# Attention followed by a Fourier mixing layer on one core: the middle channel's rank-one products on 32-row tiles of TensorE, in one visit a batch

## The chip, the cores and the metric

The kernel runs on one core of one Trainium2 chip. The metric is the device time of one execution in microseconds (us); several runs give a median. The engines are named as in the profile: PE is TensorE's matrix multiplication and PEld its weight load, DVE is VectorE, ACT is ScalarE, POOL is GpSimd, SP is SyncE, which here only issues DMAs. L1267 is line 1267 of the kernel before; the changed kernel's lines differ by up to some fifty and are named as such.

## What is computed

Eight batches (B = 8) of 576 tokens, 8 heads of 64, so 512 columns a token. Each batch goes through an attention without a token-by-token matrix, then through a Fourier mixing layer with a residual, a LayerNorm and a two-layer network, all in float32:

```python
q_s = softmax(q, axis=-1); k_s = softmax(k, axis=2)
kv = np.einsum('bhsd,bhse->bhde', k_s, v)
x = np.einsum('bhsd,bhde->bhse', q_s, kv)      # then (B, S, H*D) = 8 x 576 x 512
mixed = np.real(np.fft.fft(np.fft.fft(x, axis=1), axis=2))
u = x + mixed
un = (u - mean(u)) / sqrt(var(u) + 1e-6)
out = u + np.maximum(un @ w_ch1, 0) @ w_ch2     # 512 -> 2048 -> 512
```

## The kernel before, in words

**The two layers.** Nearly all of TensorE's time goes to the two matrix products of the network, which use Strassen's scheme of seven products per level (`ORDER`, products 1, 6, 5, 7, 2, 4, 3). `up` (L1544) makes the first layer of a batch, `down` and `deep_down` (L1641, L1671, L1760) the second. In `deep_down`, which serves the later groups, a unit of the scheme has seven products n, each 16 passes of 128 columns; product 1 and 2 go to the PSUM bank `ba`, 6, 7 and 4 to `bb`, 5 and 3 to `bc`. Each of the three banks exists once. After a product its `ends` step reads the bank: `plus` (L1678, on VectorE) adds bank and a kept sum into `u2`, `u3` or an output. The next product into `bb` can begin only when VectorE's read of the one before is done. The steps `a_step` (L1617) form the scheme's sums of left operands on VectorE, and some on GpSimd. A float32 product counts as two passes (two weight loads and two matmuls) on TensorE.

**The Fourier transform** is made of products with tables of cosines and sines. It uses the symmetries of the real transform: rows are folded, and of the 512 columns five blocks of spectrum channels remain, k = 0 to 4. Blocks 0 and 1 are cosines, 2 and 3 sines, of 128 (127) channels each; block 4 (`KT`) is the single middle channel.

- *First stage*, along the tokens: for batches 2 to 7 `blocks(b)` has, for each k, `own(k)` (L1207, the main products, 144 or 145 columns), `tails` (L1234, ten small products with 16 or 17 rows on 32-row tiles of TensorE, the last two for k = 4), and `copies` (L1246, L1249, L1250, on ScalarE) out of the PSUM tiles `two` into SBUF: `Z` for the batch's own channels, `ZT` for the rows shared by a pair of batches, and for the middle channel row 0 of `Zr` (own, 256 wide) and of `ZTr` (shared). All other rows of `Zr` and `ZTr` are zero. In L1207, `own(4)` uses 128 weight columns though one channel is wanted. Batch 0 has its own steps in the opening, batch 1 uses `block(1, k)`.
- *Second stage*, along the columns: `second()` for an own half c = 0 or 1 of the batch, or (odd batches) for the shared rows. `times` makes four products with the table `cd` (L1264) and, added into the same bank, the middle channel's product (L1267), whose left operand `Zr` or `ZTr` is 128 rows of which only row 0 isn't zero. `copy` (L1273, ScalarE) brings the sine half to SBUF, `sums` (L1281, L1282, VectorE) forms sum and difference of the halves, and `added` (L1294, L1295, VectorE) adds them to x in two halves, for each of the one or two row blocks.
- Then `norm` (L1321 and on), the transposes of the normalized rows (L1382) and the copies L1390 that lay out `unT`, the left operand of the next `up`.

**The order of the work** is written out by hand: each step has a time, the steps of all parts are sorted by it, and each engine then executes its instructions in that order (`manual_schedule`). A time decides order only; waits come from data and from buffers. The opening has a list of its own (`OPENING`), where the steps `m0` and `m1` are the second stage of batch 0. For batches 2 to 7 `timed` places it: the first stage from the start of the second layer on, and the mixes at

```python
for i, some in enumerate(mixes):
    steps += at(t + 9.7 + 1.65 * soon + 3.2 * i, some)
```

so that TensorE visits the second stage two times in even batches and three times in odd ones (in batch 7 the shared rows first), with Strassen products in between: in batches 3 and 5 the first visit comes after the 16 passes of product 1, the second in the middle of product 5, the third in the middle of product 2.

Of the kernel before, what the change touches and what calls it, by code (L numbers as in the profile page):

```python
# [40 lines left out]
F32 = mybir.dt.float32  # L41
# [5 lines left out]
P = 128  # L47
B, H, S, DH = 8, 8, 576, 64
D = H * DH
# [85 lines left out]
def paired(t):  # L135
    return t.rearrange("p (q a) -> p q a", a=2)


class _Block:
    def __init__(self, ctx, tc, q, kT, v, w1, w2, ft, cd, out):  # L140
# [27 lines left out]

        self.Zr, self.ZTr = c.tile([P, HD], F32, name="Zr"), c.tile([P, P], F32, name="ZTr")
        for t in (self.Zr, self.ZTr):  # L170
            nc.gpsimd.memset(t[:], 0.0)
        self.kb = c.tile([P, NR, 4, NC * Q], F32, name="kb")
# [427 lines left out]
    def opening(self, fetch, converted):  # L600
# [40 lines left out]
        for c in range(2):  # L641
            named(f"m{c} times,m{c} copy,m{c} sums,m{c} add0,m{c} add1", self.mix_own(0, c))
        tiles = [f"{c}{u}" for c, u in ((0, 0), (0, 1), (1, 0), (1, 1))]
# [502 lines left out]
    def block(self, b, k):  # L1146
# [26 lines left out]
        def copies():  # L1173
            pz, Z = box.pop(), self.Z[b]
            z, zt = (self.Zr[0:1], self.ZTr[0:1]) if k == KT else (Z[0:n, k, :], self.ZT[0:n, k, :])
            nc.scalar.copy(paired(z), interleaved(pz[:, NT - 1:NT - 1 + 2 * ME])[:, 0:P, :])

            at = W * (b % 2)
            nc.scalar.mul(paired(zt[:, at:at + Q]), interleaved(pz[:, 0:2 * MO])[:, 0:NT - 1, ::-1],
                          -1.0 if sines else 1.0)  # L1180
            nc.scalar.copy(paired(zt[:, at + Q:at + W]), interleaved(pz[:, 0:2 * ME])[:, NT - 2::-1, ::-1])
# [3 lines left out]
    def blocks(self, b):  # L1185
# [51 lines left out]
        def copies(k, part, copy=nc.scalar.copy):  # L1237
            n, sines, Z = {3: QD - 1, 4: 1}.get(k, P), k in (2, 3), self.Z[b]
            z, zt = (self.Zr[0:1], self.ZTr[0:1]) if k == KT else (Z[0:n, k, :], self.ZT[0:n, k, :])
            flat = box[sines][0:n].rearrange("p a n -> p (a n)")  # L1240
            odd, even = place(k, 1).start, D + place(k, 0).start

            def both(x, y, size, step=1):
# [4 lines left out]
            w = W * (b % 2)  # L1248
            nc.scalar.mul(paired(zt[:, w:w + Q]), both(even, odd, NT - 1), -1.0 if sines else 1.0)  # L1249
            nc.scalar.copy(paired(zt[:, w + Q:w + W]), both(even + NT - 1, odd + NT - 2, NT - 1, -1))  # L1250

        return own, tails, copies, early, sine

    def second(self, z, zr, adds, two=True, apart=None):

        nc, V = self.nc, self.nc.vector
        cd, box = self.cd, []

        def times():
            banks = apart() if apart else [self.acc((P, D), two)] * 2  # L1260
            parts = (1, 0, QD), (0, QD, QD + 1), (2, NN + QD - 1, QD), (3, NN, QD - 1)
            for k, at, size in (parts[2], (3, HD, QD), *parts[:2]) if apart else parts:
                rows, pm = QD - 1 if k == 3 else P, banks[k > 1]
                nc.tensor.matmul(pm[:, at:at + size], lhsT=z(k)[0:rows], rhs=cd[0:rows, at:at + size], start=True,  # L1264
                                 stop=(k != 0))
                if k == 0:
                    nc.tensor.matmul(pm[:, at:at + size], lhsT=zr(), rhs=cd[:, D:], start=False, stop=True)  # L1267
            box.extend(banks)

        def copy():  # L1270
            sn = self.sn[self.turns % 2]
            self.turns += 1
            nc.scalar.copy(paired(sn[:, 0:HD]), interleaved(box.pop()[:, HD:]))  # L1273
            box.append(sn)

        def sums():
            pm, sn = box
            two = self.halves()
            a = interleaved(pm[:, 0:2 * (QD + 1)])[:, 0:QD, :]
            for i, op in enumerate((ALU.subtract, ALU.add)):  # L1280
                V.tensor_tensor(out=paired(two[:, i * NN + 1:(i + 1) * NN]), in0=a, in1=paired(sn[:, 1:NN]), op=op)  # L1281
            V.tensor_copy(two[:, ::NN], pm[:, QD:QD + 1].to_broadcast([P, 2]))  # L1282
            box.append(two)

        steps = [(0, times), (2.6, copy), (3.6, sums)]
        for i, add in enumerate(adds):
            steps.append((5 + 1.2 * i, lambda add=add: add(box[2][:, 0:NN], box[2][:, NN:])))
        return steps
# [7 lines left out]

    def mix_shared(self, p):
        return self.second(lambda k: self.ZT[:, k, :], lambda: self.ZTr[:],
                           [lambda lo, hi: self.added(self.xshared(p), hi, lo)])

    def mix_own(self, b, c):
        s = slice(c * P, (c + 1) * P)
        adds = [lambda lo, hi: self.added(self.xpart(b, c, 0), lo, hi, of=None if b or c else self.kept), lambda lo, hi: self.added(self.xpart(b, c, 1), hi, lo, None if b else self.nc.gpsimd)]
        def apart():
# [5 lines left out]
        return self.second(lambda k: self.Z[b][:, k, s], lambda: self.Zr[:, s], adds, apart=None if b else apart)  # L1310

# [522 lines left out]
def kernel(ctx: ExitStack, tc: tile.TileContext, q, kT, v, w1, w2, ft,  # L1834
# [3 lines left out]
    def timed(t, order, g):  # L1838
# [155 lines left out]
```

## Time and profile before

| what | value |
|---|---|
| three runs | 1005.66, 1005.86, 1006.8 us; median 1005.86 us |
| profiled execution | span 1006.6 us (the profile gives no time outside its span) |
| granted clock of TensorE | 9 tenths or more in each of 40 slices |
| busy: PE, PEld, DVE, ACT, POOL | 99%, 85%, 71%, 49%, 44% of the span |
| DMA | 236.37 MB, 235 GB/s in the mean |

How to read it: the span runs from the first to the last instruction of one execution. In a timeline, a row is a run of like instructions that follow each other: start in us, length in us, engine, line, operation, output and input tiles with their shapes, and how many; in square brackets the idle time ahead of it and what ended it. Two rows of one engine can overlap, since instructions are pipelined: the pace of an engine is read from the starts, not from the lengths. The ends of PE rows are modelled.

### The profile page before, as it was taken

What the parts mean: (1) busy time and instruction counts of PE and PEld (TensorE: products, weight loads), DVE (VectorE), ACT (ScalarE), POOL (GpSimd) and SP (SyncE); (2) the same over time, 40 slices, a digit from 0 to 9 for tenths busy, and PEclk for the clock granted to TensorE, in tenths of its full rate; (3) what the DMA queues carried; (4) which work ended last, traced back from release to release, by engine and by line L of the source; (5) the groups of instructions that cost most, each with busy time, mean ns of one, the idle gap of its engine ahead of it and who ended that gap; (6) DMA issues with size and microseconds to landing.
All of it is one profiled execution on the core that took longest, in us unless ns stands there. A gap on an engine that the chain in (4) does not pass through costs nothing.

```text
span 1006.6 us, 19808 instructions
## 1 busy us (share of the span) xinstructions
PE 995.6 (99%) x7562; PEld 855.7 (85%) x7562; DVE 718.6 (71%) x1356; ACT 493.2 (49%) x1277; POOL 442.9 (44%) x445
## 2 busy tenths in 40 slices
PE   8999999999999999999999999999999999999998
PEld 6844464888888899889988998899889998998897
DVE  6898898666765887588756877688667945685563
ACT  4585642872468228832775177625772342151200
POOL 4263420357535637664655465655646450040000
PEclk9999999999999999999999999999999999999999
DMA  9987499687989666975677577847753765674573
GB/s 300 258 281 245 158 240 346 205 243 226 342 283 272 230 230 219 266 237 210 251 220 242 206 269 237 253 174 270 231 204 135 267 213 200 224 265 172 183 256 132
DMA packets 123559, 236.37 MB, mean 235 GB/s; under 512 B 24184, under 2 KB 88440, under 8 KB 112840
## 3 DMA queue, kind: packets, MB, share of 16 engines
q1 hardware_dynamic: 123096, 234.58, 71.0%
q8 instruction: 60, 0.98, 0.4%
q14 instruction: 35, 0.29, 0.1%
q10 hardware_dynamic: 288, 0.26, 0.1%
q0 software_dynamic: 80, 0.26, 0.1%
HBM read 199.94 MB, written 39.06 MB: 237 GB/s over the span
## 4 chain that ended last, share of the span: by engine, by line
PE 87%; DVE 7%; ACT 3%; DMA 1%; issue 1%; SPq 0%; POOL 0%; DVEq 0%; POOLq 0%
PE bb L1544 16%; PE ba L1544 11%; PE bc L1544 11%; PE bb L1671 10%; PE ba L1671 7%; PE bc L1671 7%; PE bb L1641 5%; PE bc L1479 2%; PE bb L1760 2%; PE two L840 2%; PE one L755 2%; PE two L1207 1%; PE two L1264 1%; PE ba L1479 1%; PE bc L1760 1%; PE ba L1760 1%
## 5 line engine op out<-in xcount | busy, mean ns | idle before, releaser
L1544 PE MATMUL bb<-unT,big 128*128 128x256 f32 x768 | 183.3, 380 | 0.0
L1544 PEld LDWEIGHTS bb<-unT,big 128*128 128x128 f32 x768 | 144.8, 190 | 20.7 <-DVE u L1514 0.7
L1556 ACT ACTIVATE big<-big 128x512 f32<-128x512 f32 x96 | 59.8, 629 | 147.6 <-DVE big L1555 141.0
L1544 PE MATMUL ba<-unT,big 128*128 128x256 f32 x512 | 123.9, 382 | 0.0
L1544 PE MATMUL bc<-unT,big 128*128 128x256 f32 x512 | 121.5, 380 | 0.1
L817 ACT ACTIVATE qT<-q 32x128 f32<-32x128 f32 x384 | 117.9, 307 | 5.9 <-DVE q L807 0.8
L1544 PEld LDWEIGHTS bc<-unT,big 128*128 128x128 f32 x512 | 96.9, 190 | 13.7 <-DVE big L1555 0.5
L1544 PEld LDWEIGHTS ba<-unT,big 128*128 128x128 f32 x512 | 95.5, 190 | 13.9 <-issue 0.5
L1514 DVE TENSOR_TENSOR u<-bb,s 128x512 f32<-128x512 f32 x66 | 45.2, 685 | 85.0 <-PE bb L1544 66.5
L1671 PE MATMUL bb<-big 128*128 128x128 f32 x848 | 103.8, 276 | 0.2 <-DVE u L1678 0.2
L1671 PEld LDWEIGHTS bb<-big 128*128 128x128 f32 x848 | 98.9, 192 | 1.0 <-DVE u L1678 1.0
L1390 POOL COPY unT<-unT 32x256 f32<-32x256 f32 x98 | 42.0, 428 | 90.2 <-DVE unT L1382 85.9
L1621 POOL TENSOR_TENSOR x<-x,big 128x512 f32<-128x512 f32 x45 | 60.9, 1368 | 46.0 <-DVE big L1678 19.7
L1617 DVE TENSOR_TENSOR big<-big 128x512 f32<-128x512 f32 x98 | 79.9, 842 | 0.0
L1671 PE MATMUL ba<-big 128*128 128x128 f32 x640 | 79.0, 276 | 0.0
L1671 PEld LDWEIGHTS ba<-big 128*128 128x128 f32 x640 | 75.0, 192 | 0.8
L1390 ACT COPY unT<-unT 32x256 f32<-32x256 f32 x126 | 50.7, 402 | 31.3 <-DVE unT L1382 29.5
L804 POOL TENSOR_TENSOR q<-q,qm 128x512 f32<-128x512 f32 x24 | 25.8, 1073 | 88.2 <-DVE qm L799 53.1
L405 POOL TENSOR_TENSOR big<-big 128x512 f32<-128x512 f32 x24 | 30.4, 1268 | 68.4 <-ACT big L1556 68.4
L1641 PE MATMUL bb<-big 128*128 128x256 f32 x256 | 58.3, 379 | 0.0
L1555 DVE TENSOR_TENSOR big<-bc,u 128x512 f32<-128x512 f32 x64 | 44.0, 688 | 17.3 <-PE bc L1544 16.4
L1641 PEld LDWEIGHTS bb<-big 128*128 128x128 f32 x256 | 48.0, 190 | 6.1
(336 smaller groups left out, 1917.9 us busy)
## 6 DMA issues: line engine op xcount, KB each, us to landing
big<-w2d SPq DMA_DIRECT2D x67, 1024.0 KB, 4.6
big<-w1s SPq DMA_DIRECT2D x64, 896.0 KB, 4.7
big<-w2s SPq DMA_DIRECT2D x16, 1024.0 KB, 4.8
big<-in_w_dram SPq DMA_DIRECT2D x21, 512.0 KB, 6.0
w2d<-big SPq DMA_DIRECT2D x42, 256.0 KB, 6.5
kb<-in_kT_dram SPq DMA_DIRECT2D x28, 320.0 KB, 7.8
q<-in_q_dram SPq DMA_DIRECT2D x28, 256.0 KB, 6.0
vt<-in_v_dram SPq DMA_DIRECT2D x84, 80.0 KB, 2.7
```

The source lines that it names most:

```text
L405: e1.tensor_tensor(out=to(4), in0=at(2), in1=at(3), op=ALU.add)
L817: nc.scalar.activation(to[t, i * Q:i * Q + Q], one, ACT.Exp)
L1390: copy(to, of)
L1514: plus = lambda t: V.tensor_tensor(out=temp(t), in0=box["bb"][:], in1=box["s1"][:], op=ALU.add)
L1544: nc.tensor.matmul(bank()[:, i, :], lhsT=w[:, WA_AT[m], k * P:(k + 1) * P], rhs=self.unT[g][:, B_AT[m], k, :], start=first and i == 0 and ...
L1555: steps = [(0, lambda: V.tensor_tensor(out=hp(i), in0=bank()[:], in1=u()[:], op=ALU.add)), (0.8, lambda: nc.scalar.activation(hp(i), hp(i) ...
L1556: (0.8, lambda: nc.scalar.activation(hp(i), hp(i), ACT.Relu))]
L1617: e.tensor_tensor(out=to(o), in0=to(x), in1=to(y), op=op)
L1621: E.tensor_tensor(out=x, in0=x, in1=tile(m), op=ALU.add)
L1641: nc.tensor.matmul(box[name][:, i, :], lhsT=h[p][:, A_AT[m], i * P:(i + 1) * P], rhs=self.stream[n][:, p, :], start=p == 0 and (m != 1 or ...
L1671: nc.tensor.matmul(box[place[n]][:, i, :], lhsT=own(m)(A_AT[n])[:, f, :], rhs=w[:, r // 2, r % 2 * P:r % 2 * P + P], start=first and f == ...
L1760: nc.tensor.matmul(bank()[:, i, :], lhsT=h[p][:, A_AT[m], i * P:(i + 1) * P], rhs=w[:, p, :], start=first and i == 0 and p == 0, stop=p == ...
```

## The change

- The three rows of the middle channel (own half 0, own half 1, shared) now stand at partitions 0, 32 and 64 of one tile `Zr`; `ZTr` is gone. Their products take one row each as left operand, which puts them on three 32-row tiles of TensorE.
- All products of a batch's second stage are made in one step, `mix`: first the four products with `cd` for each part, then the middle channel's two or three products behind each other. Its time is that of the old first visit in even batches; in odd ones it is 1.6 later, which puts it behind product 6 instead of ahead of it. The steps copy, sums and adds keep their distances, 1.6 later too in odd batches. Batch 1 makes its three parts in one step at the first one's time; batch 0 keeps two steps with one part each.
- The own halves of a batch from 2 on share one PSUM tile `two` (two banks), the shared part has another.
- In the first stage of batches 2 to 7 `own(4)` uses 32 weight columns: the odd-row product on rows 0 to 31 of the bank, the even-row one on rows 32 to 63, on two column tiles of TensorE. The two tails of k = 4 become tiles of 32 by 32.
- The copies of the middle channel are cut accordingly: four small ones for own (two in batch 1) where it was one, four for shared where it was two.

```diff
-        self.Zr, self.ZTr = c.tile([P, HD], F32, name="Zr"), c.tile([P, P], F32, name="ZTr")
+        self.Zr = c.tile([P, HD], F32, name="Zr")
+        self.Zrow = lambda i: self.Zr[i * Q:i * Q + 1, 0:P]
...
-        wide = lambda k, i: slice(cols[k][i], cols[k][i] + (QD - 1 if k == 3 else P))
+        wide = lambda k, i: slice(cols[k][i], cols[k][i] + (QD - 1 if k == 3 else Q if k == KT and b else P))
...
-        bank = lambda k, odd: box[k in (2, 3)][:QD - 1 if k == 3 else P, 1 - odd, place(k, odd)]
+        def bank(k, odd):
+            rows = slice(Q * (1 - odd), Q * (1 - odd) + Q) if k == KT and b else slice(0, QD - 1 if k == 3 else P)
+            return box[k in (2, 3)][rows, 1 - odd, place(k, odd)]
...
+            if k == KT:
+                low = box[sines][Q * (b > 0):Q * (b > 0) + 1].rearrange("p a n -> p (a n)")
+                for to, x, y, size, step in ([(self.Zrow(c), odd + NT - 1 + c * W, even + NT + c * W, W, 1) for c in range(2)] if part == "own" else
+                                             [(self.Zrow(2)[:, w:w + Q], odd, even, NT - 1, 1),
+                                              (self.Zrow(2)[:, w + Q:w + W], odd + NT - 2, even + NT - 1, NT - 1, -1)]):
...
+                    for i, (of, a) in enumerate(ends):
+                        copy(paired(to)[:, :, i], bass.AP(of.tensor, of.offset + a, [of.ap[0], [step, size]]))
+                return
...
-    def second(self, z, zr, adds, two=True, apart=None):
+    def second(self, parts):
...
-                if k == 0:
-                    nc.tensor.matmul(pm[:, at:at + size], lhsT=zr(), rhs=cd[:, D:], start=False, stop=True)
-            box.extend(banks)
+            for i, (_, row, *_) in enumerate(parts):
+                rows = slice(row * Q, row * Q + 1)
+                nc.tensor.matmul(box[i][0][:, QD:HD + 1], lhsT=self.Zr[rows, 0:P], rhs=cd[rows, D:], start=False, stop=True,
+                                 skip_group_check=True)
+
+        return [(0, times)], [self.summed(lambda i=i: box[i], adds) for i, (_, _, adds, _) in enumerate(parts)]
...
+        def half():
+            if self.phase == 1:
+                return single()
+            if not open_banks:
+                t = self.two()
+                open_banks.extend([t[:, 0, :], t[:, 1, :]])
+            return [open_banks.pop(0)] * 2
...
-        mixes = [blk.mix_own(b, c) for c in range(2)]
-        if b % 2:
-            mixes.insert(0 if b == B - 1 else 2, blk.mix_shared(b // 2))
+        times, mixes = blk.mix(b, ((2, 0, 1) if b == B - 1 else (0, 1, 2)) if b % 2 else (0, 1))
+        steps += at(t + 9.7 + 1.65 * soon + 1.6 * (b % 2), times)
         for i, some in enumerate(mixes):
-            steps += at(t + 9.7 + 1.65 * soon + 3.2 * i, some)
+            steps += at(t + 9.7 + 1.65 * soon + 3.2 * i + 1.6 * (b % 2), some)
...
-    for i, some in enumerate((blk.mix_own(1, 0), blk.mix_own(1, 1), blk.mix_shared(0))):
+    times, mixes = blk.mix(1, (0, 1, 2))
+    steps += at(t + 35.5, times)
+    for i, some in enumerate(mixes):
         steps += at(t + 35.5 + 3.4 * i, some)
```

`summed` holds the old steps copy, sums and adds, unchanged but for where they read.

More of the change, by code (lines that the diff above doesn't have):

```diff
@@ L1247, in copies @@
                 return
-            w = W * (b % 2)
             nc.scalar.mul(paired(zt[:, w:w + Q]), both(even, odd, NT - 1), -1.0 if sines else 1.0)
@@ L1252, in blocks, with summed @@
         return own, tails, copies, early, sine
-    def second(self, z, zr, adds, two=True, apart=None):
+    def second(self, parts):
         nc, V = self.nc, self.nc.vector
-        cd, box = self.cd, []
+        cd, box = self.cd, {}
         def times():
[L1260 to L1265, printed above, removed]
-                if k == 0:
-                    nc.tensor.matmul(pm[:, at:at + size], lhsT=zr(), rhs=cd[:, D:], start=False, stop=True)
-            box.extend(banks)
+            for i, (z, *_, banks) in enumerate(parts):
+                box[i] = banks = banks()
+                sizes = (1, 0, QD), (0, QD, QD + 1), (2, NN + QD - 1, QD), (3, NN, QD - 1)
+                two = banks[0] is not banks[1]
+                for k, at, size in (sizes[2], (3, HD, QD), *sizes[:2]) if two else sizes:
+                    rows, pm = QD - 1 if k == 3 else P, banks[k > 1]
+                    nc.tensor.matmul(pm[:, at:at + size], lhsT=z(k)[0:rows], rhs=cd[0:rows, at:at + size],
+                                     start=k == 1 or (two and k == 2), stop=(k != 0), skip_group_check=True)
+            for i, (_, row, *_) in enumerate(parts):
[3 more added lines that the diff above has]
+        return [(0, times)], [self.summed(lambda i=i: box[i], adds) for i, (_, _, adds, _) in enumerate(parts)]
+    def summed(self, banks, adds):
+        nc, V = self.nc, self.nc.vector
+        box = []
         def copy():
@@ L1283, in sums @@
             box.append(two)
-        steps = [(0, times), (2.6, copy), (3.6, sums)]
+        steps = [(2.6, copy), (3.6, sums)]
         for i, add in enumerate(adds):
-            steps.append((5 + 1.2 * i, lambda add=add: add(box[2][:, 0:NN], box[2][:, NN:])))
+            steps.append((5 + 1.2 * i, lambda add=add: add(box[1][:, 0:NN], box[1][:, NN:])))
         return steps
@@ L1295, in added, with mix, single, apart @@
         V.tensor_tensor(out=x[:, NN:], in0=of[:, NN:], in1=g[:, HD - 1:0:-1], op=ALU.add)
[L1297 to L1304, printed above, removed]
+    def mix(self, b, some):
+        open_banks = []
+        def single():
+            return [self.acc((P, D), True)] * 2
+        def half():
[5 more added lines that the diff above has]
+            return [open_banks.pop(0)] * 2
+        def apart(c):
             if c == 0:
@@ L1308, in apart @@
             return [t[:, 0, :], t[:, 1, :]]
-        return self.second(lambda k: self.Z[b][:, k, s], lambda: self.Zr[:, s], adds, apart=None if b else apart)
+        parts = []
+        for c in some:
+            if c == 2:
+                parts.append((lambda k: self.ZT[:, k, :], 2, [lambda lo, hi: self.added(self.xshared(b // 2), hi, lo)], single))
+                continue
+            adds = [lambda lo, hi, c=c: self.added(self.xpart(b, c, 0), lo, hi, of=None if b or c else self.kept),
+                    lambda lo, hi, c=c: self.added(self.xpart(b, c, 1), hi, lo, None if b else self.nc.gpsimd)]
+            s = slice(c * P, (c + 1) * P)
+            parts.append((lambda k, s=s: self.Z[b][:, k, s], c, adds, half if b else lambda c=c: apart(c)))
+        return self.second(parts)
     def norm(self, g):
```

26 lines of the change are left out of this document (18 added, 8 removed).

## Prediction

> **What bounds the kernel now.** I read the page first (busy shares, then the chain that ended last), then TensorE's timeline around the lines that the change touches, then VectorE's timeline beside it.
>
> ```profile
> span 1006.6 us, 19808 instructions
> ...
> PE 995.6 (99%) x7562; PEld 855.7 (85%) x7562; DVE 718.6 (71%) x1356; ACT 493.2 (49%) x1277; POOL 442.9 (44%) x445
> ...
> PE 87%; DVE 7%; ACT 3%; DMA 1%; issue 1%; SPq 0%; POOL 0%; DVEq 0%; POOLq 0%
> ```
>
> TensorE is busy 99% of the span and is 87% of the chain. Every pass taken off it is therefore worth its full pace, and every stall put on it costs its full length. VectorE's 71% is a mean; in the odd batches' second stage, below, it has no room.
>
> All sums are differences inside the profiled execution. Its span, 1006.6 us, is 0.7 us above the median of the three runs (1005.86) and just under the slowest (1006.8). I add the difference to the median. About 0.2% (2 us) is what a measurement of this kernel can tell from no change.
>
> **Part 1, the middle channel's products in the second stage.** Batch 3's three visits of TensorE:
>
> ```profile
> 351.89 0.61 PE L1264 MATMUL two<-cd,Z 128*128 128x128 f32 x4
> 352.34 0.39 PE L1267 MATMUL two<-cd,Zr 128*128 128x129 f32 x2
> 352.56 0.61 PE L1264 MATMUL two<-cd,Z 128*128 128x128 f32 x4
> 353.01 1.95 PE L1671 MATMUL bb<-big,unT 128*128 128x128 f32 x16
> ...
> 371.32 1.95 PE L1671 MATMUL bb<-big 128*128 128x128 f32 x16
> ...
> 374.89 1.98 PE L1671 MATMUL bb<-big 128*128 128x128 f32 x16
> ```
>
> The starts give paces: one product L1267 (two passes) displaces 352.56-352.34 = 0.22 us; a 128-column pass takes 0.45/4 = 0.112 us; one visit takes 353.01-351.89 = 1.12 us. There are 20 such products (two own channels in each of 8 batches, and 4 shared visits).
>
> The changed products stand on 32-row tiles, side by side. No L1267 runs that way today, but the tails L1234 do, so they price the switch of tile shape in and out:
>
> ```profile
> 348.49 0.66 PE L1207 MATMUL two<-ft,eo 128*128 128x144 f32 x4
> 349.07 1.00 PE L1234 MATMUL two<-ft,eo 17*128 17x145 f32 x20
> 350.00 2.05 PE L1671 MATMUL ba<-big 128*128 128x128 f32 x16
> ```
>
> ```profile
> 238.52 1.15 PE L1207 MATMUL two<-ft,eo 128*128 128x144 f32 x8
> 239.50 0.81 PE L1760 MATMUL bb<-big 128*128 128x256 f32 x3
> ```
>
> The pace of a 144-column pass is 0.98/8 = 0.123 us. In: the four L1207 last 349.07-348.49 = 0.58 instead of 0.49, so 0.09 more. Inside: the twenty tail passes are six rounds side by side (four tiles by two passes, twice, then two tiles by two passes), 6 x 0.123 = 0.74, and last 0.93, so 0.19 more. Out: sixteen 128-column passes last 351.89-350.00 = 1.89 instead of 16 x 0.112 = 1.79, so 0.10 more. A switch in and out thus costs 0.38 us, and a packed visit 0.38 + 2 x 0.112 = 0.60 us however many tiles it holds. The Trainium skill, "TensorEngine Tiling (Array Packing)", Tiling Modes, says that a change of tiling mode drains TensorE; it has no price for it. By the rule the switch grows with the number of visits, by a rule of tiles alone it would be nothing (second rival).
>
> - Odd batches 1, 3, 5, 7: 3 x 0.22 = 0.67 goes, 0.60 comes: -0.07 each, -0.28.
> - Even batches 2, 4, 6: 0.45 goes, 0.60 comes: +0.16 each, +0.48.
> - Batch 0 keeps two visits of one product each: 0.22 goes, 0.60 comes, +0.38 twice. They lie in the opening, where VectorE's first sums wait for the first visit (0.19 us, row below). Of the 0.76 I take +0.5, since the first visit's 0.38 goes straight into that wait and part of the second runs beside VectorE's work on the first. Ends 0 and 0.76.
>
> ```profile
> 35.40 0.76 DVE L1281 TENSOR_TENSOR eo<-tr,sn 128x256 f32<-128x256 f32 x2 [0.19 <-PE tr L1267]
> ```
>
> **Part 2, the first stage of batches 2 to 7.** The middle channel's block has two products, four passes of 0.123. On two column tiles they are two rounds: 0.25 saved. Its tails move from 32x128 to 32x32 tiles, two rounds as before. But the shape changes two more times per batch (128x128, 128x32, 32x128, 32x32, 128x128 where it was 128x128, 32x128, 128x128). Half of the 0.38 above, 0.19, is one change's mean; two would cost 0.38, and at the price of the way in alone (0.09) 0.19. So -0.06 to +0.13 per batch; I take 0, with ends -0.4 and +0.8 for six batches.
>
> **Part 3, ScalarE's copies.** The middle block's copies split (own one into four, shared two into four). ScalarE is 49% busy, and the visits start later than today in odd batches and after the same bank's copies in even ones. Cost nothing; if that cover were gone, some 0.2 us a batch.
>
> **Part 4, the order in odd batches.** This is where I see the change's largest price. The three visits of batches 3, 5, 7 become one, placed after product 6 (the first into bank bb), so the first visit comes 1.79 later and the others are pulled up. TensorE is in step again behind the third visit's old place. VectorE isn't, because its list is a fixed order:
>
> ```profile
> 355.07 0.42 DVE L1678 TENSOR_TENSOR u<-bb,s 128x256 f32<-128x256 f32 x1 [3.49 <-PE bb L1671]
> ...
> 357.34 1.49 DVE L1294 TENSOR_TENSOR x<-x,eo 128x257 f32<-128x257 f32 x1
> 358.75 1.49 DVE L1295 TENSOR_TENSOR x<-x,eo 128x255 f32<-128x255 f32 x1
> 360.16 0.41 DVE L1678 TENSOR_TENSOR u<-bb,s 128x256 f32<-128x256 f32 x1
> 360.60 0.42 DVE L1678 TENSOR_TENSOR big<-bc,u 128x256 f32<-128x256 f32 x1
> 360.95 0.42 DVE L1294 TENSOR_TENSOR x<-x,eo 128x257 f32<-128x257 f32 x1
> ...
> 370.27 0.41 DVE L1678 TENSOR_TENSOR u<-bb,s 128x256 f32<-128x256 f32 x1
> ...
> 374.35 0.41 DVE L1678 TENSOR_TENSOR u<-bb,s 128x256 f32<-128x256 f32 x1
> ```
>
> From the read of product 6 (355.07) on VectorE doesn't idle until after the last read shown: no row of its timeline up to there shows a wait. Changed, TensorE's order is: product 6 from 351.89 to 353.68; the visit, 24 passes x 0.112 + 0.60 = 3.3, to 356.98; products 5 and 7 to 360.55. Product 6's read came 0.27 behind its last start's end (355.07 against 353.01+1.79 = 354.80), so the read of 7 comes at 360.82, 0.66 later than today (360.16). Meanwhile, between the end of its read of 6 (354.3) and 360.82, VectorE has only two steps L1617 and the first sums in its list, some 2 us of work in 6.5: the visit is over too late for more. One pair of adds (L1294, L1295), which stood before the read of 7, now stands behind it: 2 x 0.35, 0.7 (0.35 is the pace from 360.60 to 360.95, and the operation at 360.95 is an add that wasn't held, with the same 0.42). Those two took 1.49 each today, because a GpSimd operation ran beside them:
>
> ```profile
> 356.89 3.06 POOL L1617 TENSOR_TENSOR big<-big 128x512 f32<-128x512 f32 x2 [2.97 <-DVE big L1617]
> ```
>
> I take this hold as gone, since GpSimd's two operations wait for VectorE's steps L1617, which now run right behind the read of 6 while VectorE then idles. So everything behind moves by 0.66 + 0.7 = 1.36: the reads of 370.27 and 374.35 to 371.63 and 375.71. TensorE needs the first done by 371.32-0.07 = 371.25 and the second by 374.82, and they are done 0.35 later than they start: 371.98 and 376.06. That is a stall of 0.7, then 0.5 more, 1.2 in all. A stall has a tail: in batch 7 today
>
> ```profile
> 798.56 2.05 PE L1671 MATMUL bb<-big 128*128 128x128 f32 x16
> 800.45 1.95 PE L1671 MATMUL bc<-big 128*128 128x128 f32 x16
> ```
>
> the product that had to wait lasts 1.89 instead of 1.79, 0.10 more. Two stalls: 1.2 + 0.2 = +1.4 for batch 3, with Part 1's -0.07 already in it. Batch 5 likewise:
>
> ```profile
> 571.38 0.42 DVE L1678 TENSOR_TENSOR u<-bb,s 128x256 f32<-128x256 f32 x1
> ...
> 585.60 0.41 DVE L1678 TENSOR_TENSOR u<-bb,s 128x256 f32<-128x256 f32 x1
> ```
>
> ```profile
> 563.59 0.61 PE L1264 MATMUL two<-cd,Z 128*128 128x128 f32 x4
> ...
> 586.59 1.95 PE L1671 MATMUL bb<-big 128*128 128x128 f32 x16
> ```
>
> Read of 7: 563.59 + 1.79 + 3.3 + 3.57 + 0.27 = 572.52, 1.14 late; with the adds 1.84; the read of 585.60 is done at 585.60 + 1.84 + 0.35 = 587.79 instead of being needed at 586.59: +1.2, with the tails +1.4. Batch 7 has another order (shared first) and one stall already; I take +1.2 for it, by its two neighbours. Ends for each of the three: 0 (VectorE finds the time) and +2.5 (the hold stays for one add). No DMA is issued by a moved step, and weight slots come free in step again behind the old third visit. Even batches keep their first visit's place, and batch 1 has no such list of reads beside it: no stall there.
>
> **Sum:** -0.07 (batch 1) + 0.48 + 0.5 + 0 + 0 + (1.4 + 1.4 + 1.2) = +4.9 us: 1005.86 + 4.9 = **1010.8 us**. Its own ends, from those of the parts: about 1008 to 1013.5.
>
> **Rivals.**
>
> - VectorE keeps step (17%). What counts is TensorE alone: -0.28 + 0.48 + 0.5 = +0.7, 1006.6. For it: VectorE idles some 4 us in the changed order (2 us of work in 6.5), and steps off the list could slip in. Against: its order is fixed, and reads of bb stand behind everything else on it. It decides whether the read moved to 371.63 ends before 371.25.
> - Switching costs nothing (7%), the other side, **faster**. Then 20 x 0.22 = 4.46 goes and nine visits of 0.22 come, -2.4, and -0.25 x 6 = -1.5 in the first stage: -3.9, about 1002, if VectorE keeps step too. It decides at (4.46 - 2.02)/9 = 0.27 us for a switch in and out: above that, nine visits eat all that the second stage saves. Against: L1234 shows 0.38. The Trainium skill, "TensorE: Matmul & The Clock Gate", Part 3, gives packed products a span of one product plus some 4 ns per further tile, with no term for a switch; that is this case, and the rows above speak against it.
> - GpSimd's hold stays (10%): its operations fall beside VectorE's adds behind the read of 7, 1.07 more for each held add, two in batch 3, one or two in 5 and 7: +4.9 + 4 x 1.07 = +9, about 1015.
> - The tiles don't run side by side (8%): each further product costs its 0.22 after all, 4 x 0.45 + 3 x 0.22 = +2.4 on top: 1013.
>
> **How the numbers follow.** Forecast 58%, rivals 17, 7, 10 and 8. Faster by over 0.2%: 7% (the second rival). Within 0.2%: 15% of the first rival and 3% of the forecast, where the stalls are half as long and the opening hides its part: 18%. Slower: 75%. The range runs from the first rival less its own ends, 1006, to 1014, which takes in the forecast and the fourth rival; out are the second and most of the third.
>
> **What the changed profile would show.** Right: a gap of 0.6 between the last own or shared product of a visit and the next Strassen product; TensorE waits for L1725 (the read, L1678 before) two times in each of batches 3, 5, 7, in all some 4 us; VectorE idle 2 us ahead of the first sums and again ahead of the read of product 7; first sums of the opening 0.4 later. Wrong: no such waits (first rival); own(4) followed by no gap and a packed visit of 0.25 (second); adds of 1.49 behind the read of 7 (third); rank-1 products 0.22 apart (fourth).

## The result and the profile after

The changed kernel is **slower by 0.69%** (95% interval 0.57% to 0.81%, ratio 1.0069): 1014.0 us median of four runs (1013.63 to 1014.37) beside 1006.33 us (1005.66 to 1008.37) for four runs of the kernel before. 0.69% is 6.9 us, 5.7 to 8.2 by the interval; the two medians alone lie 7.7 us apart. Forecast were +4.9 us and 1010.8 us, with 1014 as the upper end of the range; so the direction and the place were right and the size fell short. The time stands on the very edge of the range, and outside the 1008 to 1013.5 us that the prediction worked out from the ends of its own parts. The half microsecond by which the range is wider is all that takes it in, and that is luck. As a loss, 6.9 us lies inside the parts' own ends (about 2 to 7.6 us above 1005.86).

The page of the changed kernel, its busy shares, its chain and the rows of the second layer's products into `bb` (columns: busy us and mean ns; idle us of the engine just ahead, and what ended most of it):

```profile
span 1012.0 us, 19838 instructions
...
PE 998.2 (99%) x7562; PEld 851.9 (84%) x7562; DVE 714.1 (71%) x1356; ACT 500.7 (49%) x1313; POOL 443.6 (44%) x444
...
PE 84%; DVE 11%; DMA 2%; ACT 1%; issue 1%; SPq 0%; POOL 0%; DVEq 0%; POOLq 0%
...
L1718 PE MATMUL bb<-big 128*128 128x128 f32 x848 | 104.9, 277 | 3.2 <-DVE u L1725 3.0
...
L1718 PEld LDWEIGHTS bb<-big 128*128 128x128 f32 x848 | 98.9, 192 | 5.7 <-DVE u L1725 5.5
```

The last of these rows on the page of the kernel before:

```profile
L1671 PEld LDWEIGHTS bb<-big 128*128 128x128 f32 x848 | 98.9, 192 | 1.0 <-DVE u L1678 1.0
```

Here one sees the loss by name. TensorE has the same 7562 instructions and is as busy as before, but VectorE's share of the chain grew from 7% to 11%, and the weight loads of the products into `bb` (L1718, L1671 before) wait 5.5 us for VectorE's read `u` (L1725), where it was 1.0 us.

**Where along the span.** The table sets the starts of the same product (the first of each batch's first layer) side by side; the differences were taken before rounding. Beside the first profile of before it needs a second one (run e0, below), since the first one's start was 0.5 us later; its products lie 0.8 to 0.9 us behind the second's from 174 us on, without a change.

| start of the first layer of | before, second profile | changed | changed less before | growth in the stretch, and whose second stage lies in it |
|---|---|---|---|---|
| batch 0 | 42.16 | 43.28 | +1.13 | |
| batch 1 | 173.94 | 174.10 | +0.16 | opening and batch 1: +0.16 |
| batch 2 | 283.95 | 284.30 | +0.35 | batch 2: +0.19 |
| batch 3 | 390.40 | 391.60 | +1.20 | batch 3: +0.85 |
| batch 4 | 495.75 | 498.08 | +2.33 | batch 4: +1.14 |
| batch 5 | 601.77 | 605.33 | +3.55 | batch 5: +1.22 |
| batch 6 | 707.12 | 711.81 | +4.69 | batch 6: +1.14 |
| the rows shared by pairs | 814.15 | 820.66 | +6.51 | batch 7: +1.82 |
| (last Strassen product) | 1001.36 | 1007.87 | +6.51 | |

The second stage of a batch lies in the second layer of the batch before it. From batch 3 on each batch loses 0.9 to 1.8 us, and after batch 7's second stage nothing is lost any more.

Batch 3 of the changed kernel, TensorE's timeline:

```profile
351.32 1.95 PE L1718 MATMUL bb<-big,unT 128*128 128x128 f32 x16
353.11 1.95 PE L1286 MATMUL two<-cd,Z 128*128 128x128 f32 x16
354.89 1.06 PE L1286 MATMUL two<-cd,ZT 128*128 128x128 f32 x8
355.88 0.50 PE L1290 MATMUL two<-cd,Zr 1*128 1x129 f32 x6
356.31 2.05 PE L1718 MATMUL bc<-big,unT 128*128 128x128 f32 x16
...
368.91 1.95 PE L1718 MATMUL bc<-big 128*128 128x128 f32 x16
371.03 2.05 PE L1718 MATMUL bb<-big 128*128 128x128 f32 x16 [0.17 <-DVE u L1725]
...
375.12 2.05 PE L1718 MATMUL bb<-big 128*128 128x128 f32 x16 [0.25 <-DVE u L1725]
```

and VectorE's beside it:

```profile
353.38 0.43 DVE L1725 TENSOR_TENSOR u<-bb,s 128x256 f32<-128x256 f32 x1 [2.40 <-PE bb L1718]
353.72 1.28 DVE L1664 TENSOR_TENSOR big<-big 128x512 f32<-128x512 f32 x2
356.82 0.76 DVE L1311 TENSOR_TENSOR eo<-two,sn 128x256 f32<-128x256 f32 x2 [1.82 <-ACT sn L1303]
357.49 0.15 DVE L1312 COPY eo<-two 128x2 f32<-128x2 f32 x1
360.18 0.42 DVE L1725 TENSOR_TENSOR u<-bb,s 128x256 f32<-128x256 f32 x1 [2.54 <-PE bb L1718]
```

One visit, 24 passes with `cd` and 6 of the middle channel, lasts 356.31-353.11 = 3.20 us, and the product behind it 0.10 more. VectorE idles 1.8 us until the visit is over and another 2.5 us in front of the read of product 7, with the adds of the first sums standing behind that read. Later it is late for two reads, and TensorE waits in front of 371.03 and 375.12. In a row like these the idle time in brackets is less than what is lost: from the product at 368.91 to the one at 371.03 there are 2.12 us where sixteen passes take 1.79, so 0.33 is lost there, then 0.10 in the product itself.

In batch 4 something else comes first, the visit's own wait (TensorE, then ScalarE):

```profile
457.10 2.05 PE L1718 MATMUL ba<-big 128*128 128x128 f32 x16
459.32 2.05 PE L1286 MATMUL two<-cd,Z 128*128 128x128 f32 x16 [0.16 <-ACT ZT L1270]
461.30 0.49 PE L1290 MATMUL two<-cd,Zr 1*128 1x129 f32 x4
461.72 2.05 PE L1718 MATMUL bb<-big,unT 128*128 128x128 f32 x16
```

```profile
457.94 0.86 ACT L1260 COPY Zr<-two 1x64 f32<-1x64 f32 x4
...
459.06 0.21 ACT L1270 COPY ZT<-two 127x32 f32<-127x32 f32 x1
```

The four copies of the middle channel's own row last 0.86 us (one copy of 0.36 before) and stand ahead of the copies that release the sines' bank. That bank is the one into which the visit writes. Product 1 in front of it starts at 457.10, behind the switch back from the tails, and would be followed 1.89 us later (as in the prediction's rows), at 458.99: 0.33 lost, and 0.10 more in the visit's first passes, as behind any wait.

### The profile page after: what moved, and what is told of

The parts are those of the page before. It is cut to its first block, busy times and chain, and to the rows that moved or that the text cites. A ratio compares the mean times of both kernels' runs of the same rounds, so it can differ in the third digit from the quotient of the medians.

```text
span 1012.0 us, 19838 instructions
## 1 busy us (share of the span) xinstructions
PE 998.2 (99%) x7562; PEld 851.9 (84%) x7562; DVE 714.1 (71%) x1356; ACT 500.7 (49%) x1313; POOL 443.6 (44%) x444
## 4 chain that ended last, share of the span: by engine, by line
PE 84%; DVE 11%; DMA 2%; ACT 1%; issue 1%; SPq 0%; POOL 0%; DVEq 0%; POOLq 0%
PE bb L1591 16%; PE ba L1591 11%; PE bc L1591 11%; PE bb L1718 9%; PE bc L1718 6%; PE bb L1688 5%; PE ba L1718 5%; PE bc L1526 2%; PE bb L1807 2%; DVE big L1664 2%; PE two L841 2%; PE one L756 2%; PE two L1286 1%; PE two L1215 1%; PE ba L1526 1%; PE bc L1807 1%
## 5 line engine op out<-in xcount | busy, mean ns | idle before, releaser
L1718 PE MATMUL bb<-big 128*128 128x128 f32 x848 | 104.9, 277 | 3.2 <-DVE u L1725 3.0
L1718 PEld LDWEIGHTS bb<-big 128*128 128x128 f32 x848 | 98.9, 192 | 5.7 <-DVE u L1725 5.5
L1664 DVE TENSOR_TENSOR big<-big 128x512 f32<-128x512 f32 x98 | 78.5, 830 | 0.0
L1718 PE MATMUL ba<-big 128*128 128x128 f32 x640 | 78.5, 276 | 0.0
L1718 PEld LDWEIGHTS ba<-big 128*128 128x128 f32 x640 | 74.8, 192 | 1.2 <-issue 1.1
```

The costliest lines, as they stand in the source:

```text
L1664: e.tensor_tensor(out=to(o), in0=to(x), in1=to(y), op=op)
L1718: nc.tensor.matmul(box[place[n]][:, i, :], lhsT=own(m)(A_AT[n])[:, f, :], rhs=w[:, r // 2, r % 2 * P:r % 2 * P + P], start=first and f == ...
```

## The experiments

Two theories stood at the outset. **A, the fixed order:** the loss is waits, for VectorE's reads and for ScalarE's copies, that the change brings about in lists whose order is fixed. **B, the switch:** the loss is what TensorE pays for changing tile shape. After the first four runs a third one came up: **C, the place:** the visit's place alone makes the reads late, whatever VectorE does meanwhile.

**e0_before_again**, the kernel before, unchanged.

> The kernel before, profiled a second time. Both theories: the same time as before. It tells which waits of the first profile belong to that execution alone. Between 98 and 112 us the first profile has 1.2 us more between its layer products than the changed kernel's has, at places that the change does not touch (a wait for q at L985, 0.5 us, and one for xs at L840, 0.2 us). If those are of the one execution, this profile's span is about 1004 to 1005.5 us, and the true loss of the change is 1 to 2 us larger than the two first spans say (5.4).

Ratio 0.9997 (0.9987 to 1.0007), span 1005.8 us. The forecast of which waits would be gone was wrong. Both are there again:

```profile
103.70 0.68 PE L840 MATMUL acc<-pairs,qT 64*64 64x64 f32 x28 [0.19 <-ACT xs L1080]
...
110.46 0.66 PE L985 MATMUL tr<-ident,q 128*128 128x128 f32 x4 [0.53 <-DVE q L957]
```

The changed kernel has neither row. Its opening ends 0.6 to 1.1 us later (43.28 against 42.70 and 42.16), and q then doesn't have to be waited for: most of what the opening loses is given back at these two places. A second profile shows what one can't see in one: which waits are the kernel's own.

**e1_rows128**: the visit as it is, without row tiles in the second stage.

```diff
-                rows = slice(row * Q, row * Q + 1)
-                nc.tensor.matmul(box[i][0][:, QD:HD + 1], lhsT=self.Zr[rows, 0:P], rhs=cd[rows, D:], ...
+                nc.tensor.matmul(box[i][0][:, QD:HD + 1], lhsT=self.Zr[:, row * P:(row + 1) * P], rhs=cd[:, D:], ...
```

> Keeps the single visit, its place, the order and the first stage; only the middle channel's two or three products of the second stage are 128-row products again, so the second stage changes no tile shape. Theory A (the fixed order: the loss is mostly waits behind VectorE's list in batches 3 to 7): opening 0.6 less, even batches 0.16 less each, odd ones 0.07 more each, the waits stay: about 0.8 us below the changed kernel, still some 6 us above before. Theory B (the loss is what TensorE pays for changing tile shape): the loss goes, within 1 us of before.

Ratio 1.0066 (1.0048 to 1.0084), 1013.93 us beside 1007.04: the loss stays without a single row tile in the second stage. Theory B falls for the second stage. It falls for the first stage too, which keeps its two further changes of shape here: batch 2, which has that stage and no other wait, loses 0.01 us where the changed kernel loses 0.19. The last product starts only 0.16 us earlier than in the changed kernel, where theory A had expected 0.8; the opening's 0.66 us are again given back by 174 us.

**e2_visit_first**: the visit of odd batches ahead of product 6.

```diff
-        steps += at(t + 9.7 + 1.65 * soon + 1.6 * (b % 2), times)
+        steps += at(t + 9.7 + 1.65 * soon, times)
         for i, some in enumerate(mixes):
-            steps += at(t + 9.7 + 1.65 * soon + 3.2 * i + 1.6 * (b % 2), some)
+            steps += at(t + 9.7 + 1.65 * soon + 3.2 * i, some)
```

> Keeps the tiles; in batches 3, 5 and 7 the one visit and its sums stand 1.6 earlier in the list, which puts the visit ahead of product 6 (where the first visit was before). VectorE then has the first sums and the first adds ahead of the read of product 7. Theory A: the waits for the read of bb in batches 3, 5, 7 (0.9, 1.2 and some 2 us) go, 3 to 4 us below the changed kernel, 3 to 4 above before. Theory B: as the changed kernel, 7 us above before, since the number of switches is the same.

Ratio 1.0100 (1.0083 to 1.0117), 1017.04 us beside 1007.04: three microseconds worse, where three to four better were expected. VectorE's timeline of batch 3 says why:

```profile
356.98 0.42 DVE L1725 TENSOR_TENSOR u<-bb,s 128x256 f32<-128x256 f32 x1 [6.11 <-PE bb L1718]
357.32 0.75 DVE L1311 TENSOR_TENSOR eo<-two,sn 128x256 f32<-128x256 f32 x2
357.98 0.15 DVE L1312 COPY eo<-two 128x2 f32<-128x2 f32 x1
358.05 1.28 DVE L1664 TENSOR_TENSOR big<-big 128x512 f32<-128x512 f32 x2
359.25 1.49 DVE L1324 TENSOR_TENSOR x<-x,eo 128x257 f32<-128x257 f32 x1
360.66 1.48 DVE L1325 TENSOR_TENSOR x<-x,eo 128x255 f32<-128x255 f32 x1
```

I had put the sums where VectorE is free in time, but in its list they stand behind the read of product 6, which now comes 3.60 us later than in the changed kernel (356.98 against 353.38). It idles 6.1 us in front of that read, though the sums could have run, and the adds are then held at 1.49 us by GpSimd (0.42 alone). That is compatible with A and with C.

**e3_copies_later**: in even batches the middle copies behind those that release the bank.

```diff
-                steps.append((t + soon + 7.8 + 0.2 * i + 1.0 * j, lambda k=k, part=part: copies(k, part)))
+                steps.append((t + soon + 7.8 + 0.2 * i + 1.0 * j + (0.5 if k == KT and j == 0 and b % 2 == 0 else 0), lambda k=k, part=part: copies(k, part)))
```

> As the changed kernel, but in even batches ScalarE's four copies of the middle channel's own row come after the copies that release the sines' bank, not before them. Theory A: the visits of batches 4 and 6 no longer wait for that bank (0.3 us each, with 0.1 of refill), and VectorE's reads behind them come less late: 0.8 to 1.6 us below the changed kernel. Theory B: no difference.

The time alone tells little: 1013.43 us, ratio 1.0070 (1.0048 to 1.0093). The trace does: against the changed kernel the distance falls by 0.43 us at the visit of batch 4 and 0.40 at that of batch 6, and by nothing elsewhere from batch 2 on (from +0.83 us behind batch 1 to +0.08 at the end); no wait of these visits for a copy is left. In the profiled execution 0.7 us were lost between 43 and 165 us, where the two kernels are the same, which covers it.

**e5_apart**: the tiles kept, each part in a visit of its own again.

```diff
-        times, mixes = blk.mix(b, ((2, 0, 1) if b == B - 1 else (0, 1, 2)) if b % 2 else (0, 1))
...
+        for i, c in enumerate(((2, 0, 1) if b == B - 1 else (0, 1, 2)) if b % 2 else (0, 1)):
+            times, (some,) = blk.mix(b, (c,))
+            steps += at(t + 9.7 + 1.65 * soon + 3.2 * i, times + some)
```

> Keeps the row tiles, the column tiles and the copies, but every part of the second stage has a visit of its own at the place it had before: 20 visits with one 32-row product each instead of 9. It prices the switch of tile shape in the second stage, in the order of before. By the switch that the changed kernel's trace shows (about 0.4 us a visit), 18 visits from batch 1 on lose 0.4 each, some 7 us, and the opening next to nothing, with no new wait for VectorE's reads in batches 3 to 7. If a switch cost nothing here, the time would be that of before.

Ratio 1.0094 (1.0078 to 1.0109), 1016.72 us beside 1007.75. At eleven of its visits the distance to before grows by 0.38 or 0.39 us each; at the first visits of batches 3 to 7 it grows by some 0.4 more, in front of which TensorE waits for ScalarE's copies. With them the loss is 9 us where 7 were expected. These waits thus come from the copies, of which there are more now, and not from the single visit. A second visit of batch 3:

```profile
358.06 1.06 PE L1286 MATMUL two<-cd,Z 128*128 128x128 f32 x8
359.05 0.48 PE L1290 MATMUL two<-cd,Zr 1*128 1x129 f32 x2
359.46 1.16 PE L1718 MATMUL bc<-big,unT 128*128 128x128 f32 x8
360.46 1.95 PE L1718 MATMUL bb<-big 128*128 128x128 f32 x16
```

The visit lasts 1.40 us (1.12 before), and the eight passes behind it 1.00 instead of 0.89: 0.39 more. The switch costs what the tails had shown. VectorE's reads are waited for no more than before (0.8 us in all): with the order of before, the added waits for L1725 are gone. So those come from the single visit.

**e6_sums_early**, **e7_all_early**, **e8_mixed**: TensorE's order as changed, VectorE's list changed.

```diff
-            steps += at(t + 9.7 + 1.65 * soon + 3.2 * i + 1.6 * (b % 2), some)
+            steps += at(t + 9.7 + 1.65 * soon + (3.0 if b % 2 else 3.2) * i - 0.9 * (b % 2), some)
```

(e7: -2.4 for batches 4 and 6 too, and the copies of e3; e8: as e7, `Zr` with 128 rows in even batches and 32-row tiles in odd ones only.)

> The changed kernel with the same order on TensorE; in batches 3, 5 and 7 only the copies, sums and adds of the second stage stand 2.5 earlier in the list, so that VectorE runs the first sums, the first adds and the second sums while it waits for product 7, not behind its read. Theory A (VectorE's list: it idles while work that it could do stands behind the read of a product): the waits of TensorE for the read of bb in batches 3, 5, 7 go, 3 to 4 us below the changed kernel. Theory C (the place of the visit alone makes the reads late, whatever VectorE does meanwhile): no gain.

> As e6_sums_early, and in batches 4 and 6 the sums and adds 2.4 earlier, and in even batches ScalarE's middle copies behind those that release the sines' bank. Theory A: the waits of batches 4 and 6 go as well (0.9 us each), 5 to 6 us below the changed kernel and 0.5 to 1.5 above before, which is what TensorE itself pays. Theory C: like e3_copies_later, 0.8 below the changed kernel.

> As e7_all_early, with the middle channel's products of the even batches 0, 2, 4, 6 as 128-row products behind the others (two of 0.22 cost less than a switch in and out), and on row tiles only in the odd batches, where three stand beside each other. Theory A and the prices of the trace: 0.2 us a batch below e7_all_early in batches 2, 4, 6, so 0.6 less, and within 0.5 us of before: no version of the idea that saves anything a measurement can tell.

e6: ratio 1.0078 (1.0063 to 1.0093), no gain over the changed kernel as a whole. By batches it divides: batch 7 loses nothing (the distance is 8.70 us ahead of it and 8.68 behind) where the changed kernel loses 1.82, but batches 3 and 5 get a new wait of 1.7 us, for the read of product 7. e7: 1.0057 (1.0042 to 1.0073), batches 4 and 6 lose 0.3 each instead of 1.1. e8: 1.0045 (1.0032 to 1.0059). All three missed what was expected of them (3 to 4 us gained, 5 to 6 gained, and a time within 0.5 us of before). VectorE's and GpSimd's timelines of e7 in batch 3:

```profile
357.83 0.68 DVE L1664 TENSOR_TENSOR big<-big 128x512 f32<-128x512 f32 x1
358.43 0.42 DVE L1324 TENSOR_TENSOR x<-x,eo 128x257 f32<-128x257 f32 x1
358.76 1.49 DVE L1325 TENSOR_TENSOR x<-x,eo 128x255 f32<-128x255 f32 x1
360.18 0.68 DVE L1664 TENSOR_TENSOR big<-big 128x512 f32<-128x512 f32 x1
360.78 0.41 DVE L1324 TENSOR_TENSOR x<-x,eo 128x257 f32<-128x257 f32 x1
361.12 1.49 DVE L1325 TENSOR_TENSOR x<-x,eo 128x255 f32<-128x255 f32 x1
```

```profile
358.58 1.39 POOL L1664 TENSOR_TENSOR big<-big 128x512 f32<-128x512 f32 x1 [4.97 <-DVE big L1664]
361.00 1.32 POOL L1664 TENSOR_TENSOR big<-big 128x512 f32<-128x512 f32 x1 [1.03 <-DVE big L1664]
```

My new list had pushed VectorE's two steps L1664 behind the first sums. GpSimd waits for each of them, and its operation then holds the next add for 1.07 us. That is the mechanism of the prediction's third rival, here made by the experiment itself; it costs two times 1.07 us ahead of the read of 7.

**e9_lists**, **e10_lists_mixed**: in batches 3 and 5 those two steps first, then the sums and adds (e10 with 128-row products in even batches, as e8).

```diff
+            if b in (3, 5):
+                dts = ((13.9, 14.9, 15.05, 15.1), (14.0, 15.2, 19.5, 20.7), (20.3, 21.3, 22.7))[i]
+                steps += [(t + dt, step) for dt, (_, step) in zip(dts, some)]
+            else:
...
```

> As e7_all_early with all its tiles and the same order on TensorE, but in batches 3 and 5 VectorE's steps L1664, for which GpSimd waits, come first again, right behind the read of product 6, and only then the first sums, the first four adds and the second sums, all ahead of the read of product 7. Theory A with GpSimd's hold (in e7_all_early two adds of batch 3 took 1.49 us each because those steps stood behind the sums): the read of product 7 is no more than 0.3 us late, TensorE's wait for it (1.7 us in batches 3 and 5) goes, and the later ones stay away: 3 to 3.6 us below e7_all_early, 1.5 to 2.5 above before. Theory C (the place of the visit makes the reads late): no gain over e7_all_early.

> As e9_lists, with 128-row products in the even batches 0, 2, 4, 6 and row tiles in the odd ones only, as in e8_mixed. By the prices measured so far (a switch in and out 0.38 us, a 128-row product 0.22) it lies 0.5 to 0.8 us below e9_lists and within 1.5 us of before. If it is below before, by no more than 0.3 us.

e9: ratio 1.0031 (1.0019 to 1.0042), 1010.57 us beside 1007.58; e10: 1.0020 (1.0011 to 1.0030). More than half of the loss is gone while TensorE's order is that of the changed kernel, so theory C falls and A stands. e9 is 3.0 us above before and e10 1.8, where at most 2.5 and 1.5 were expected. Batches 3 and 5 still lose 0.75 and 1.08 us, and VectorE's timeline of e9 shows idle time that was left:

```profile
363.57 0.42 DVE L1725 TENSOR_TENSOR big<-bb,s 128x256 f32<-128x256 f32 x1 [1.49 <-PE bb L1718]
```

**e11_lists_full**, **e12_full_mixed**: the second half's adds ahead of that read too.

```diff
-                dts = ((13.9, 14.9, 15.05, 15.1), (14.0, 15.2, 19.5, 20.7), (20.3, 21.3, 22.7))[i]
+                dts = ((13.9, 14.9, 15.05, 15.1), (14.0, 15.2, 17.6, 18.6), (20.3, 21.3, 22.7))[i]
```

> As e9_lists, with the second half's four adds of batches 3 and 5 ahead of the read of product 4: in e9_lists VectorE idles 1.5 us in front of that read while the adds stand behind it, and TensorE still waits 0.9 us for two later reads in batch 3 and 1.0 us in batch 5. Theory A: these waits go as well, 1.5 to 2 us below e9_lists, 0.5 to 1.5 above before, which is what the tiles themselves cost (0.1 to 0.2 in each of batches 2, 4, 6, little in the opening, some hundredths less in odd batches). Theory C: no gain.

> As e11_lists_full, with 128-row products in the even batches and row tiles in the odd ones only. 0.5 to 1 us below e11_lists_full; within 0.7 us of before on either side. This is the best that the idea has to give by the prices measured here.

e11: ratio 1.0021 (1.0012 to 1.0031), 1009.15 us beside 1007.02; e12: 1.0009 (1.0000 to 1.0018), 1008.09 us beside the same 1007.02. Batch 3 of e11 now loses 0.12 us and batch 5 0.48 (differences of the starts, as in the table above). The waits of the weight loads for VectorE's read, of the changed kernel and of e11:

```profile
PEld bb L1718 <- DVE u L1725: 5.5, 12, 2.0
```

```profile
PEld bb L1718 <- DVE u L1725: 1.5, 5, 0.4
```

From 6.9 us to 2.1 us by the lists of VectorE and ScalarE alone (at most 1.5 were expected of e11); e12, without the tiles in even batches, lies another 1.1 us lower by the medians. The two traces show 0.5 us of that in batches 2, 4 and 6; the rest lies in the first 174 us, where batch 0 has no tiles either and where the two profiles of before differ by 0.8 us. No version beats the kernel before, and the best one, e12, is at most 0.18% behind it. The expectation for e12 (within 0.7 us) was met only by its interval (0 to 1.8 us), not by its mean (0.9).

## Why the prediction was right, and where its sum fell short

- **Price of a switch, 0.38 us:** right. e5_apart measured 0.38 to 0.39 for a visit with one tile. A visit of three tiles saves 3.2 + 0.10 against three visits of 1.12, 0.05 (forecast 0.07), and an even batch's costs 0.19 (batch 2, the one without other waits; forecast 0.16). The second rival (a switch costs nothing) is excluded by e5. The fourth (tiles not side by side) is excluded by the passes themselves: one tile's, two tiles' and three tiles' take 0.41, 0.42 and 0.43 us up to the next product (359.46-359.05 in e5, 461.72-461.30, 356.31-355.88).
- **First stage, 0:** right; batch 2, which contains it, loses 0.19 in all, what its visit alone accounts for, and in e1, with the first stage as changed, 0.01.
- **Opening, +0.5:** too much in the end. From the opening's first visit to the first layer it takes 0.73 us more (43.28-33.65 against 42.16-33.26), the upper end of the forecast's 0 to 0.76, but opening and batch 1 together lose 0.16 by 174 us, since two waits of the kernel before (0.2 and 0.5 us) are absorbed. The term looked at the opening alone and not at the next wait behind it.
- **Part 3, ScalarE's copies at nothing:** this step failed. I had named as cover that the visits of even batches come "after the same bank's copies"; that is the very wait. The middle copies take 0.86 instead of 0.36 us and stand ahead of the release: 0.33 + 0.10 us in each of batches 4 and 6. The price that the prediction gave for lost cover, 0.2 us a batch, was half of it. e3 removes 0.43 and 0.40. In the odd batches the cover held: their visits start later.
- **Part 4, odd batches, 1.4 + 1.4 + 1.2 = 4.0:** the mechanism was right, and so was the sum: 0.85 + 1.22 + 1.82 = 3.89. The shares were not, and that they add up is luck: batch 3 came out 0.55 below its forecast, batch 5 0.18 below, batch 7 0.62 above. Batch 3 has the two stalls at the two reads that were named, 0.33 and 0.41 (forecast 0.7 and 0.5), with up to 0.1 of refill each. Counted from the start of product 1, the read of 7 is 0.59 later than in the second profile of before (forecast 0.66), but the two later reads are 0.85 later and not 1.36: VectorE's step L1664 just ahead of them (369.27) takes 1.37 us where it took 1.67, which is most of the difference. No add of batches 3 and 5 is held in the changed kernel, as the prediction took it. Batch 7, taken "by its two neighbours", has its own: two adds held by GpSimd at 1.50 and 1.49 us ahead of the read, so that TensorE waits 1.9 us at once:

```profile
800.10 2.05 PE L1718 MATMUL bb<-big 128*128 128x128 f32 x16 [1.78 <-DVE u L1725]
```

```profile
794.28 1.50 DVE L1325 TENSOR_TENSOR x<-x,eo 128x255 f32<-128x255 f32 x1
795.70 1.49 DVE L1324 TENSOR_TENSOR x<-x,eo 128x257 f32<-128x257 f32 x1
```

```profile
794.17 2.74 POOL L1668 TENSOR_TENSOR x<-x,big 128x512 f32<-128x512 f32 x2 [7.08 <-issue]
```

  Held adds behind the read of 7 were the third rival's sign. Of the odd batches it came true in this one alone. Beside the same two GpSimd operations one add was held in the kernel before (789.51 in its second profile), so one hold behind that read is new; one ahead of it (780.27 there) is gone.

- **"Even batches keep their first visit's place: no stall there":** this failed too, and it is the largest miss. The visit keeps its place but not its length: it is 2.4 us where the first one was 1.1, so product 6 and its read come later, and the sums stand behind that read. VectorE idles 5.2 us in front of it in batch 4, and TensorE is late at the end (488.85 to 490.83 is 1.98 us, 0.19 more than sixteen passes):

```profile
463.88 0.42 DVE L1725 TENSOR_TENSOR u<-bb,s 128x256 f32<-128x256 f32 x1 [5.22 <-PE bb L1718]
...
464.82 0.74 DVE L1311 TENSOR_TENSOR eo<-two,sn 128x256 f32<-128x256 f32 x2
```

```profile
488.85 1.95 PE L1718 MATMUL bc<-big 128*128 128x128 f32 x16
490.83 2.05 PE L1718 MATMUL bb<-big 128*128 128x128 f32 x16
```

  The read ahead of 490.83 had itself waited 0.52 us for ScalarE's copy `s`, as in the kernel before; that copy stands behind steps of ScalarE that VectorE releases, so VectorE's lateness reaches TensorE by way of ScalarE there.

  Batches 4 and 6 lose 0.5 us each in waits for L1725, and with the copies and the visit 1.14 each where 0.16 was forecast. In e7, with the sums ahead of the read and the copies of e3, these batches lose 0.3 each, of which the visit's tiles are 0.19. Batch 2, with other products beside it, loses nothing of the kind.
- **The first rival** (VectorE keeps step, +0.7) didn't happen, but e11 and e12 show that one comes near it by writing the lists anew: +2.1 and +0.9.

So the forecast's 4.9 us and the trace's 6.5 (6.51 at the last product) differ by two terms above all: the even batches 2, 4 and 6 cost 2.5 us where 0.48 was forecast, and opening with batch 1 cost 0.16 where 0.43 was.

What stays open: e12's trace loses 1.7 us against the second profile of before from 174 us on. Of this 0.89 are lost in one go at 539 us, where TensorE waits in a first layer for the load of weights (`big` from `w1s`), a place that the change doesn't touch; e11's trace has no such wait there. The other 0.8 us stand at the visits' batches, 0.47 of them in batch 5, and in the odd batches e11 loses the same, so they are the change's own. Whether the wait at 539 us belongs to the kernel or to that one execution wasn't settled.

## What to carry to other kernels

When work is pulled together on the busiest engine, follow the lists of the others: the engine that reads the results may stand idle in front of a later read, with work behind that read which it could do, and pay for it several products later. A shorter sequence on TensorE is worth nothing if its price, here 0.38 us for each switch of tile shape in and out, equals what it saves; count visits, not products. And cost a batch by its own list, not by its neighbour's.

## What the hardware showed that I had not expected

An add on VectorE with both operands in SBUF took 0.42 us alone and 1.48 to 1.50 us while a GpSimd operation of the same kind ran beside it, and in the rows shown here each GpSimd operation held one such add. The Trainium skill, "SBUF — State Buffer", SBUF: two separate sides, says that a VectorE operation with two SBUF inputs and a GpSimd operation that reads SBUF take one pair of ports in turn, for a whole instruction each; the traces agree: in e7 the add of 358.76 ends at 360.25, 0.28 us behind the GpSimd operation that ends at 359.97. Where GpSimd's operation starts is decided by VectorE's own list, since it waits for steps in it; putting those steps first (e9) took two such holds of 1.07 us out of the way ahead of the read of 7. By its trace e9 loses 2.5 us less in batches 3 and 5 than e7, which differs from it only in the lists of these two batches (1.9 and 2.5 us in e7, 0.75 and 1.08 in e9).

A wait on TensorE costs more than its idle time. The prediction had this from one product of batch 7; in the changed kernel sixteen passes took 1.89 instead of 1.79 us behind a wait (371.03 to 372.92) and behind a switch of tile shape (461.72 to 463.61).
